# Attention with landmark softmax, then a SiLU MLP: M on 64x32 parts of the array, C v by column halves, and a different order in the first batch

## The chip, the core and the metric

The kernel runs on one core of one Trainium2 chip. The metric is the device time of one execution, in microseconds (us). Engines are named as in the profile: PE is TensorE (matmuls), PEld its weight loads, DVE is VectorE, ACT is ScalarE, POOL is GpSimd. A comparison gives medians, and a ratio with its 95% interval.

## The reference

```python
# B=8 batches, H=8 heads, S=576 tokens, D=64; m=32 landmarks; then an MLP 512 -> 2048 -> 512 on 4608 tokens
q_lm = q.reshape(B, H, m, S // m, D).mean(axis=3)      # k_lm likewise
A  = softmax(q    @ k_lm^T / 8)
Bm = softmax(q_lm @ k_lm^T / 8)
C  = softmax(q_lm @ k^T    / 8)
Z  = Bm^T / (norm1(Bm) * norminf(Bm))
for _ in range(6):
    Z = 2 * Z - Z @ Bm @ Z
attn = A @ Z @ C @ v
h = x @ w_in;  out = (h * sigmoid(h)) @ w_out          # x: attn with the heads side by side
```

## The kernel before

The kernel never forms `attn`. Per batch it makes M, that is (Z C v) of every head times the head's 64 rows of `w_in` (a 32x2048 block for each head), and the first layer is then A times M. The batches overlap: while the first layer of batch b runs (`l1_unit`, tile `h_ps`), the attention of batch b+1 is made in steps between its units, and the second layer (`ops`) of earlier tokens fills in. The tiles `h_ps`, `m_ps` and three of the attention's share a pool of two buffers of two PSUM banks each (`big`); `lm_ps`, `w_ps`, `ns_ps` and others share two buffers of one bank (`small`).

```python
    # v tile: 10 columns blocks of 384; blocks 1..8 are the heads, 0 and 9 are ones (they give the softmax sums)
    vslots = [vp.tile([VP, 10, VI * Dh], BF, ...) for i in range(NV)]
    ...
    idf = constp.tile([128, 128], FP, ...)            # identity in f32, then cast
    nc.vector.memset(idf, 1.0)
    nc.gpsimd.affine_select(out=idf, in_=idf, ...)
    nc.vector.tensor_copy(out=idb, in_=idf)
    ...
    for g in range(NG):                               # selectors, in the pool of lm_ps
        sel_ps = smps.tile([128, 1024], BF, tag="small", name="sel_ps")
        nc.tensor.transpose(out=sel_ps[0:2 * H, 0:128], in_=selm[:, g]..., identity=idb)
        nc.vector.tensor_copy(out=sel[:, g, :], in_=sel_ps[0:2 * H, 0:128])
    ...
    # attn(b): landmark sums of q and k together
        for j in range(J):
            mm(lm_ps[:, 0:256]..., idb, qk[:, :, :, j, :], start=(j == 0), stop=(j == J - 1))
    ...
        def c_times_v(g):                             # once for each half of the heads
            for i in range(VI):
                mm(w_ps[:, 0:320], cts[g][:, i, :], vs[:, 5 * g:5 * g + 5, i * Dh:(i + 1) * Dh], ...)
            nc.scalar.copy(out=wsb[:, g, :], in_=w_ps[:, off:off + 256])
            nc.vector.reciprocal(out=wrec[:, g:g + 1], in_=w_ps[:, so:so + 1])
    ...
        for g in range(NG):                           # M: K=128 rows (two heads, masked), 64 columns
            for f2 in range(2):
                m_ps = big("m_ps")
                for ff in range(2):
                    for p in range(2):
                        mm(m_ps[64 * p:64 * p + 64, ff, :], zt[:, 2 * g + p, :], w_in_sb[:, 2 * g + p, f * 512:(f + 1) * 512])
                nc.scalar.copy(out=m_sb[:, g, f2 * 1024:(f2 + 1) * 1024], in_=m_ps...)
    ...
    def l1_unit(b, dc):
        h_ps = big("h_ps")
        ... 4 matmuls of 288 columns ...
        nc.scalar.activation(out=sig, in_=h_ps[:, :, 0:HS2], func=AF.Tanh, scale=0.5)
        nc.vector.scalar_tensor_tensor(out=gT[...], in0=sig, scalar=1.0, in1=h_ps[:, :, 0:HS2], op0=OP.add, op1=OP.mult)
```

The softmax here doesn't subtract the row's maximum and nothing guards it: scores larger than these inputs give would overflow.

Of the kernel before, what the change touches and what calls it, by code (L numbers as in the profile page):

```python
# [7 lines left out]
FP = mybir.dt.float32  # L8
BF = mybir.dt.bfloat16
AF = mybir.ActivationFunctionType  # L10
OP = mybir.AluOpType
# [4 lines left out]
def kernel(  # L16
# [9 lines left out]
    nc = tc.nc  # L26
    B, H, S, Dh = q.shape
    L = 32
    J = S // L
# [3 lines left out]
    NG = 2  # L33
    VA, VI = 3, 6
    VP = VA * L
# [3 lines left out]
    constp = ctx.enter_context(tc.tile_pool(name="constp", bufs=1))  # L39
    natp = ctx.enter_context(tc.tile_pool(name="natp", bufs=2))  # L40
    vp = ctx.enter_context(tc.tile_pool(name="vp", bufs=1))
    qtp = ctx.enter_context(tc.tile_pool(name="qtp", bufs=2))
    smp = ctx.enter_context(tc.tile_pool(name="smp", bufs=2))
# [9 lines left out]
    def big(nm):  # L53
        return bigp.tile([128, 2, 512], FP, tag="big", name=nm)

    def small(nm):
        return smps.tile([128, 512], FP, tag="small", name=nm)

    def mm(out_ap, lhsT, rhs, start=True, stop=True):
        nc.tensor.matmul(out=out_ap, lhsT=lhsT, rhs=rhs, start=start, stop=stop,  # L60
                         skip_group_check=True)


    w_in_sb = constp.tile([128, 4, DFF], BF, tag="w_in_sb", name="w_in_sb")
    w_out_sb = constp.tile([128, NDC, DMODEL], BF, tag="w_out_sb", name="w_out_sb")
    NV = 2
    vslots = [vp.tile([VP, 10, VI * Dh], BF, tag=f"v{i}", name=f"v{i}") for i in range(NV)]
    qk_t = [None] * B

    def load_qk(b):  # L70
# [7 lines left out]
    def load_v(b):  # L78
        vs = vslots[b % NV]
        for a in range(VA):  # L80
            nc.gpsimd.dma_start(
                out=vs[a * L:(a + 1) * L, 1:9, :],
                in_=v[b].rearrange("h (l a x) d -> a l h (x d)", l=L, a=VA)[a])

    def load_w_in():
        for fc in range(4):
            nc.gpsimd.dma_start(out=w_in_sb[:, fc, :],
                                in_=moe_w_in[fc * 128:(fc + 1) * 128, :])

    def load_w_out():  # L90
        for c in range(4):
# [4 lines left out]
    load_qk(0)  # L96


    idf = constp.tile([128, 128], FP, tag="idf", name="idf")
    nc.vector.memset(idf, 1.0)  # L100
    nc.gpsimd.affine_select(out=idf, in_=idf, compare_op=OP.is_equal, fill=0.0, base=0,
                            pattern=[[-1, 128]], channel_multiplier=1)
    idb = constp.tile([128, 128], BF, tag="idb", name="idb")
    nc.vector.tensor_copy(out=idb, in_=idf)
    hmask = constp.tile([128, 4, L], BF, tag="hmask", name="hmask")
    nc.vector.memset(hmask, 0.0)
    for a in range(4):
# [10 lines left out]
    for g in range(NG):  # L118
        sel_ps = smps.tile([128, 1024], BF, tag="small", name="sel_ps")
        nc.tensor.transpose(out=sel_ps[0:2 * H, 0:128],  # L120
                            in_=selm[:, g].rearrange("p t h -> p (t h)"), identity=idb)
        nc.vector.tensor_copy(out=sel[:, g, :], in_=sel_ps[0:2 * H, 0:128])  # L122
    pmask = constp.tile([128, 2, L], BF, tag="pmask", name="pmask")
    nc.vector.memset(pmask, 0.0)
    for a in range(2):
        nc.vector.memset(pmask[64 * a:64 * (a + 1), a, :], 1.0)
    for i in range(NV):
        nc.vector.memset(vslots[i][:, 0, :], 1.0)
        nc.vector.memset(vslots[i][:, 9, :], 1.0)

    def bc(ap, n, axis):

        shape = list(ap.shape)
        shape.insert(axis, n)
        return ap.unsqueeze(axis).to_broadcast(shape)
# [5 lines left out]
    def attn(b):  # L141
        qk = qk_t[b]
        vs = vslots[b % NV]


        lm_ps = small("lm_ps")
        for j in range(J):
            mm(lm_ps[:, 0:256].rearrange("p (t g d) -> p t g d", t=2, g=NG), idb,
               qk[:, :, :, j, :], start=(j == 0), stop=(j == J - 1))
            if j == 8:  # L150
                yield
        lm = smp.tile([128, 256], BF, tag="lm", name="lm")
        nc.scalar.copy(out=lm, in_=lm_ps[:, 0:256])  # L153

# [3 lines left out]
        def tp(t, g):  # L158
# [4 lines left out]
            else:  # L163
                for c in range(2):
# [8 lines left out]
                                op=OP.mult)  # L173
# [9 lines left out]
        for g in range(NG):  # L183
            for c in range(2):
                mm(sb_ps[:, g * L:(g + 1) * L], LB(0, g, c), LT(1, g, c),
                   start=(c == 0), stop=(c == 1))
# [24 lines left out]
        for g in range(NG):  # L211
# [6 lines left out]
            out=st[:, :, 0:128], in0=f0_ps[:, 0:256].rearrange("p (g x) -> p g x", g=NG),  # L218
            in1=bc(nrm, 128, 2), op=OP.mult)
# [49 lines left out]
        def a_rec_t(rhl):  # L269
            rt_ps = smps.tile([128, 1024], BF, tag="small", name="rt_ps")  # L270
            for ci, (c0, c1) in enumerate(CH):
                n = c1 - c0
                nc.tensor.transpose(out=rt_ps[0:2 * H, c0:c1],
                                    in_=rhl[0:n, ci].rearrange("p t h -> p (t h)"),
                                    identity=idb[0:n, 0:n])
            rt = smp.tile([2 * H, S], BF, tag="rt", name="rt")
            nc.scalar.copy(out=rt, in_=rt_ps[0:2 * H, 0:S])
            return rt

        def a_norm(g, rt):  # L280
            rb = big("rb_ps")
            for hf in range(2):
                mm(rb[:, hf, 0:HS2], sel[:, g, :], rt[:, hf * HS2:(hf + 1) * HS2])
            nc.vector.tensor_tensor(  # L284
                out=etn[:, g, :].rearrange("p (f x) -> p f x", f=2),
                in0=ets[g].rearrange("p (f x) -> p f x", f=2), in1=rb[:, :, 0:HS2], op=OP.mult)

        cts = [None] * NG
# [10 lines left out]
                                 in_=c_ps[0:VP, :, 0:384], func=AF.Exp, scale=sc / J)  # L299
            cts[g] = ct  # L300

        wsb = smp.tile([128, NG, 256], BF, tag="wsb", name="wsb")
        wrec = smp.tile([128, NG], FP, tag="wrec", name="wrec")

        def c_times_v(g):
            w_ps = small("w_ps")
            for i in range(VI):
                mm(w_ps[:, 0:320], cts[g][:, i, :],
                   vs[:, 5 * g:5 * g + 5, i * Dh:(i + 1) * Dh],
                   start=(i == 0), stop=(i == VI - 1))  # L310
            off, so = (64, 0) if g == 0 else (0, 256)
            nc.scalar.copy(out=wsb[:, g, :], in_=w_ps[:, off:off + 256])  # L312
            nc.vector.reciprocal(out=wrec[:, g:g + 1], in_=w_ps[:, so:so + 1])

        st = ns_iter(st, False)
        yield
# [12 lines left out]
        rec = a_sums()  # L329
        st = ns_iter(st, False)  # L330
        yield
        c_times_v(0)
        rt = a_rec_t(rec)
        yield
        st = ns_iter(st, False)
        yield
        a_norm(0, rt)
        c_times_v(1)
        yield
        st = ns_iter(st, True)  # L340
        yield
# [2 lines left out]
        qbd = smp.tile([128, NG, 4, L], BF, tag="qbd", name="qbd")  # L344
        for g in range(NG):
            nc.vector.scalar_tensor_tensor(
                out=qbd[:, g], in0=bc(st[:, g, 128:SW], 4, 1), scalar=wrec[:, g:g + 1],
                in1=hmask, op0=OP.mult, op1=OP.mult)
        zt_ps = small("zt_ps")
        for g in range(NG):  # L350
            for p in range(2):
                mm(zt_ps[:, (2 * g + p) * 64:(2 * g + p + 1) * 64],
                   wsb[:, g, 128 * p:128 * p + 128],
                   qbd[:, g, 2 * p:2 * p + 2, :].rearrange("p a l -> p (a l)"))
        zt = smp.tile([128, 4, 64], BF, tag="zt", name="zt")
        nc.vector.tensor_tensor(  # L356
            out=zt, in0=zt_ps[:, 0:256].rearrange("p (c x) -> p c x", c=4),
            in1=bc(pmask.rearrange("p a l -> p (a l)"), 4, 1), op=OP.mult)
        yield
        m_sb = mp.tile([128, NG, DFF], BF, tag="m", name="m")  # L360
        m_t[b] = m_sb
        for g in range(NG):
            for f2 in range(2):
                m_ps = big("m_ps")
                for ff in range(2):
                    f = 2 * f2 + ff
                    for p in range(2):
                        mm(m_ps[64 * p:64 * p + 64, ff, :], zt[:, 2 * g + p, :],
                           w_in_sb[:, 2 * g + p, f * 512:(f + 1) * 512])
                nc.scalar.copy(out=m_sb[:, g, f2 * 1024:(f2 + 1) * 1024],  # L370
                               in_=m_ps.rearrange("p f x -> p (f x)"))
                yield



# [38 lines left out]


    load_v(0)
    load_w_in()
    load_qk(1)
    load_v(1)
    load_w_out()  # L420
    for _ in attn(0):
        pass
    for b in range(B):
# [12 lines left out]
        for i, u in enumerate(l1):  # L436
            units.append(u)
            want = (i + 1) * len(l2) // len(l1)
            while n2 < want:
                units.append(l2[n2])  # L440
                n2 += 1
        gen = attn(b + 1) if b + 1 < B else iter(())
        NST = 26
        done = 0
# [8 lines left out]
        if b + 2 < B:  # L453
            load_v(b + 2)
# [33 lines left out]
```

## Time and profile before

| kernel before | |
|---|---|
| median of 4 runs | 322.64 us (322.13 to 324.32) |
| span of the profiled run, mean granted clock | 320.7 us, 0.984 |
| PE, DVE, ACT busy | 90%, 64%, 53% |
| M: matmuls, busy | 128 of 512 columns, 21.5 us |
| C v: matmuls, busy | 96 of 320 columns, 16.4 us |

The page of the kernel before. First line: span. Then each engine's busy time with its share and number of instructions; then two rows of the span in 40 slices, busy tenths of PE and the granted clock in tenths; then the chain of waits by engine and by line.

```profile
span 320.7 us, 5155 instructions
PE 287.7 (90%) x2007; PEld 162.4 (51%) x2042; DVE 205.0 (64%) x434; ACT 169.8 (53%) x269; POOL 31.0 (10%) x53
...
PE   0366989989999999999999999999999999999990
...
PEclk9999699999999999999999999999999999999997
...
PE 79%; DVE 11%; ACT 4%; DMA 2%; issue 2%; POOL 0%; ACTq 0%; DVEq 0%; POOLq 0%
PE ops L60 36%; PE h_ps L60 18%; PE m_ps L60 6%; PE lm_ps L60 5%; PE w_ps L60 4%; DVE gT L387 3%; PE c_ps L60 3%; DMA qk<-in_q_dram 2%; PE ns_ps L60 2%; PE sa_ps L60 2%; DVE qT L160 2%; PE rb_ps L60 1%; ACT sig L385 1%; DVE qT L165 1%; DVE lmbd L172 1%
```

PE is at 9 tenths in every slice from the tenth (72 us) on but the last: that stretch is held by PE. The clock has no record before 17.1 us; the row shows that time as full speed, but it was not, as the next timeline tells. M and C v (`m_ps`, `w_ps`) have 6% and 4% of the chain.

Groups of the kernel before. Columns: line, engine, operation, out<-in, rows*columns of the array, shapes, count | busy us, mean ns of one | idle us before, and the releaser.

```profile
L370 ACT CAST m<-m_ps 128x1024 bf16<-128x1024 f32 x32 | 32.2, 1013 | 18.0 <-PE m_ps L60 17.5
...
L60 PE MATMUL m_ps<-w_in_sb,zt 128*64 128x512 bf16 x128 | 21.5, 421 | 0.8 <-DVE zt L356 0.8
...
L60 PE MATMUL w_ps<-v_97,ct 96*128 96x320 bf16 x48 | 8.2, 300 | 0.0
L60 PE MATMUL w_ps<-v_96,ct 96*128 96x320 bf16 x48 | 8.2, 300 | 0.0
```

A mean of 421 ns for an M matmul is a latency, not a cost: matmuls are pipelined. The cost is read from starts. PE's timeline of the kernel before around one M group (start us, duration us, what, count):

```profile
91.17 0.62 PE L60 MATMUL m_ps<-w_in_sb,zt 128*64 128x512 bf16 x4
91.73 0.39 PE L60 MATMUL lm_ps<-qk,idb 128*128 128x256 bf16 x2
```

The group of four starts at 91.17 us and the next matmul at 91.73. In the trace the four starts are 91.172, 91.175, 91.412 and 91.415: two pairs on the two column halves, each pair streaming together.

The head in the timeline of the kernel before:

```profile
9.70 1.38 DVE L160 STREAM_TRANSPOSE qT<-qk 128x1152 bf16<-128x1152 bf16 x1 [0.74 <-DMA qk<-in_q_dram]
...
12.92 0.19 DVE L104 CAST idb<-idf 128x128 bf16<-128x128 f32 x1
...
13.16 0.37 PE L120 MATMUL sel_ps<-idb,selm 128*16 128x128 bf16 x2 [13.16 <-DVE idb L104]
...
13.46 0.34 DVE L122 COPY sel<-sel_ps 16x128 bf16<-16x128 bf16 x2 [0.35 <-PE sel_ps L120]
13.73 3.75 PE L60 MATMUL lm_ps<-qk,idb 128*128 128x256 bf16 x18 [0.20 <-DVE sel L122]
...
19.15 0.26 PE L60 MATMUL sb_ps<-lmT,lmbd 128*128 128x32 bf16 x4 [1.67 <-DVE lmbd L172]
```

The selector transposes on PE need the bf16 identity; its cast stands on DVE behind six transposes which wait for k and q, and so the landmark sums start at 13.73 us. Their starts are 213 ns apart for 256 columns (3.75 us for all 18); later in the same trace such starts are 109 ns apart, so they ran at half the clock.

### The profile page before, as it was taken

How to read it: one execution, taken by the hardware profiler on the slowest of the kernel's cores; microseconds unless marked ns; L12 is line 12 of the kernel's file. 1: busy time of each engine (PE TensorE's matmuls, PEld its weight loads, DVE VectorE, ACT ScalarE, POOL GpSimd, SP SyncE). 2: the span in 40 equal slices, each digit the busy share in tenths (PEclk: the TensorE clock that was granted, in tenths of full speed). 3: DMA queues.
4: the chain of work that ended last, by engine and by line, in shares of the span. 5: the costliest groups of instructions: out<-in, count | busy, mean ns of one | idle time of the engine just before them, and what ended most of it. 6: DMA issues, size and time to landing. Idle time of an engine off the chain costs nothing.

```text
span 320.7 us, 5155 instructions
## 1 busy us (share of the span) xinstructions
PE 287.7 (90%) x2007; PEld 162.4 (51%) x2042; DVE 205.0 (64%) x434; ACT 169.8 (53%) x269; POOL 31.0 (10%) x53
## 2 busy tenths in 40 slices
PE   0366989989999999999999999999999999999990
PEld 0243455546555754666455753666465654555440
DVE  5557589998978696589737794576437663455000
ACT  1041665676557665766474746565645747555110
POOL 7323212100101020000201020000000000000000
PEclk9999699999999999999999999999999999999997
DMA  6999999572168106180617334100011101112122
GB/s 120 209 213 205 205 208 183 73 145 65 37 105 145 53 23 119 48 156 31 106 38 142 86 58 80 49 20 21 29 38 51 46 8 37 55 41 60 50 81 68
DMA packets 18345, 28.13 MB, mean 88 GB/s; under 512 B 912, under 2 KB 9104, under 8 KB 18320
## 3 DMA queue, kind: packets, MB, share of 16 engines
q0 software_dynamic: 13568, 18.35, 33.9%
q1 hardware_dynamic: 4752, 9.44, 10.3%
q8 instruction: 16, 0.26, 0.3%
q14 instruction: 9, 0.07, 0.1%
HBM read 36.70 MB, written 9.44 MB: 144 GB/s over the span
## 4 chain that ended last, share of the span: by engine, by line
PE 79%; DVE 11%; ACT 4%; DMA 2%; issue 2%; POOL 0%; ACTq 0%; DVEq 0%; POOLq 0%
PE ops L60 36%; PE h_ps L60 18%; PE m_ps L60 6%; PE lm_ps L60 5%; PE w_ps L60 4%; DVE gT L387 3%; PE c_ps L60 3%; DMA qk<-in_q_dram 2%; PE ns_ps L60 2%; PE sa_ps L60 2%; DVE qT L160 2%; PE rb_ps L60 1%; ACT sig L385 1%; DVE qT L165 1%; DVE lmbd L172 1%
## 5 line engine op out<-in xcount | busy, mean ns | idle before, releaser
L60 PE MATMUL ops<-w_out_sb,gT 128*128 128x512 bf16 x541 | 143.4, 380 | 1.8 <-issue 0.5
L387 DVE SCALAR_TENSOR_TENSOR gT<-sig,h_ps 128x576 bf16<-128x576 bf16 x128 | 94.7, 746 | 58.9 <-ACT sig L385 58.5
L385 ACT ACTIVATE sig<-h_ps 128x576 bf16<-128x576 f32 x128 | 82.4, 650 | 47.9 <-PE h_ps L60 44.5
L60 PE MATMUL h_ps<-etn,m 128*128 128x288 bf16 x512 | 84.3, 286 | 3.0 <-DVE gT L387 2.6
L60 PEld LDWEIGHTS <-gT 128*128 128x128 bf16 x576 | 53.0, 98 | 46.6 <-issue 8.0
L60 PEld LDWEIGHTS <-m 128*128 128x128 bf16 x512 | 47.6, 97 | 34.0 <-issue 11.3
L370 ACT CAST m<-m_ps 128x1024 bf16<-128x1024 f32 x32 | 32.2, 1013 | 18.0 <-PE m_ps L60 17.5
L403 ACT ACTIVATE ost<-ops 128x512 f32<-128x512 f32 x36 | 21.4, 598 | 24.6 <-PE ops L60 24.4
L165 DVE STREAM_TRANSPOSE qT<-qk 128x576 bf16<-128x576 bf16 x32 | 23.9, 758 | 3.3 <-DMA qk<-in_k_dram 2.1
L233 DVE SCALAR_TENSOR_TENSOR st<-st,ns_ps 128x320 bf16<-128x320 bf16 (+1 forms) x48 | 20.8, 434 | 6.4 <-PE ns_ps L60 6.1
L60 PE MATMUL lm_ps<-qk,idb 128*128 128x256 bf16 x144 | 22.1, 297 | 0.3 <-DVE sel L122 0.2
L160 DVE STREAM_TRANSPOSE qT<-qk 128x1152 bf16<-128x1152 bf16 x16 | 21.7, 1358 | 0.7 <-DMA qk<-in_q_dram 0.7
L60 PE MATMUL m_ps<-w_in_sb,zt 128*64 128x512 bf16 x128 | 21.5, 421 | 0.8 <-DVE zt L356 0.8
L60 PEld LDWEIGHTS <-idb 128*128 128x128 bf16 x144 | 14.6, 105 | 8.3 <-issue 4.0
L298 ACT ACTIVATE ct<-c_ps 96x768 bf16<-96x768 f32 x16 | 12.9, 806 | 7.0 <-PE c_ps L60 7.0
L60 PE MATMUL ns_ps<-st 128*128 128x160 bf16 (+1 forms) x96 | 13.8, 224 | 2.0 <-DVE st L233 1.3
L153 ACT CAST lm<-lm_ps 128x256 bf16<-128x256 f32 x8 | 3.0, 372 | 22.7 <-PE lm_ps L60 22.7
L60 PE MATMUL c_ps<-lmbd,qT 128*96 128x128 bf16 x192 | 14.2, 219 | 0.2 <-ACT et L250 0.2
L60 PEld LDWEIGHTS <-qT 128*96 128x96 bf16 x192 | 13.3, 123 | 1.9 <-issue 0.4
L312 ACT CAST wsb<-w_ps 128x256 bf16<-128x256 f32 x16 | 5.9, 371 | 14.5 <-PE w_ps L60 8.2
L284 DVE TENSOR_TENSOR etn<-et,rb_ps 128x576 bf16<-128x576 bf16 x16 | 12.0, 747 | 1.3 <-PE rb_ps L60 1.1
L250 ACT ACTIVATE et<-sa_ps 128x576 bf16<-128x576 f32 x16 | 10.4, 648 | 4.3 <-PE sa_ps L60 4.2
(81 smaller groups left out, 178.1 us busy)
## 6 DMA issues: line engine op xcount, KB each, us to landing
out_dram<-ost SPq DMA_DIRECT2D x32, 256.0 KB
qk<-in_k_dram POOLq DMA_DIRECT2D x8, 576.0 KB, 6.0
qk<-in_q_dram POOLq DMA_DIRECT2D x8, 576.0 KB, 9.0
v_96<-in_v_dram POOLq DMA_DIRECT2D x12, 192.0 KB, 8.0
v_97<-in_v_dram POOLq DMA_DIRECT2D x12, 192.0 KB, 7.0
w_in_sb<-in_moe_w_in_dram POOLq DMA_DIRECT2D x4, 512.0 KB, 12.9
w_out_sb<-in_moe_w_out_dram POOLq DMA_DIRECT2D x4, 512.0 KB, 16.8
out_dram<-ost SPq DMA_DIRECT2D x8, 128.0 KB
```

What stands on the lines that cost most here:

```text
L60: nc.tensor.matmul(out=out_ap, lhsT=lhsT, rhs=rhs, start=start, stop=stop, skip_group_check=True)
L160: nc.vector.transpose(out=qT[:, 0, g].rearrange("p c j l -> p j c l"), in_=qk[:, 0, g].rearrange("p j (c x) -> p j c x", c=2))
L165: nc.vector.transpose(out=qT[:, 1, g, c].rearrange("p (i a) l -> p a i l", a=VA), in_=qk[:, 1, g].rearrange("p (a i) (c x) -> p a i c x", ...
L233: nc.vector.scalar_tensor_tensor(out=st2[:, :, lo:SW], in0=st[:, :, lo:SW], scalar=2.0, in1=ns_ps[:, 0:NG * SW].rearrange("p (g x) -> p g ...
L250: nc.scalar.activation(out=et.rearrange("p (f x) -> p f x", f=2), in_=sa[:, :, 0:HS2], func=AF.Exp, scale=sc / J)
L284: nc.vector.tensor_tensor(out=etn[:, g, :].rearrange("p (f x) -> p f x", f=2), in0=ets[g].rearrange("p (f x) -> p f x", f=2), in1=rb[:, :, ...
L298: nc.scalar.activation(out=ct.rearrange("p (f x) y -> p f (x y)", f=2), in_=c_ps[0:VP, :, 0:384], func=AF.Exp, scale=sc / J)
L312: nc.scalar.copy(out=wsb[:, g, :], in_=w_ps[:, off:off + 256])
L370: nc.scalar.copy(out=m_sb[:, g, f2 * 1024:(f2 + 1) * 1024], in_=m_ps.rearrange("p f x -> p (f x)"))
L385: nc.scalar.activation(out=sig, in_=h_ps[:, :, 0:HS2], func=AF.Tanh, scale=0.5)
L387: nc.vector.scalar_tensor_tensor(out=gT[:, dc, o:o + S].rearrange("p (f x) -> p f x", f=2), in0=sig, scalar=1.0, in1=h_ps[:, :, 0:HS2], op ...
L403: nc.scalar.activation(out=ost, in_=ops, func=AF.Copy, scale=0.5)
```

## The change

The intents are: M on eight 64x32 parts of the array at once, so that a group of eight matmuls streams once instead of two pairs streaming one after the other; C v on two column halves, so that fewer columns are spent on heads that a row does not need (192 in place of 320); no masking of `zt`; the identity written directly in bf16; and for batch 0 the sums of k ahead of those of q, as k lands first. For the eight parts to be distinct, the second group of heads has its row halves swapped, in `w_in_sb` and in `wsb`. The reciprocal broadcast (tile `rb_ps`, K=16 rows) is the same in both kernels.

```diff
-    vslots = [vp.tile([VP, 10, VI * Dh], BF, ...) for i in range(NV)]
+    vslots = [vp.tile([VP, H, 2, VI * Dh], BF, ...) for i in range(NV)]     # ones behind each head
...
+            if fc < 2: ... as before
+            else:                                                           # row halves swapped
+                for r in range(2):
+                    nc.gpsimd.dma_start(out=w_in_sb[64 * r:64 * r + 64, fc, :],
+                        in_=moe_w_in[fc * 128 + 64 * (1 - r):fc * 128 + 64 * (2 - r), :])
...
-    idf = constp.tile([128, 128], FP, ...)   ... memset, affine_select, tensor_copy to idb
+    idb = constp.tile([128, 128], BF, ...)   ... memset, affine_select
...
-        nc.vector.memset(vslots[i][:, 0, :], 1.0)
-        nc.vector.memset(vslots[i][:, 9, :], 1.0)
+        nc.vector.memset(vslots[i][:, :, 1, :], 1.0)
...
+        if b == 0:
+            for t in (1, 0):
+                for j in range(J):
+                    mm(lmv[:, t], idb, qk[:, t, :, j, :], start=(j == 0), stop=(j == J - 1))
+                yield
+        else: ... as before
...
-        def c_times_v(g): ... 6 matmuls of 320 columns, one copy, one reciprocal; called at two steps
+        def c_times_v():
+            for g in range(NG):
+                for i in range(VI):
+                    for p in range(2):
+                        mm(wv[64 * p:64 * p + 64, g], cts[g][:, i, 64 * p:64 * p + 64],
+                           vsl[:, 8 * g + 4 * p:8 * g + 4 * p + 3, i * Dh:(i + 1) * Dh], ...)
+            nc.scalar.copy(out=wsb[:, 0], in_=wv[:, 0, 0:3:2, :])
+            for r in range(2):
+                nc.scalar.copy(out=wsb[:, 1, r, :], in_=wv[:, 1, 2 - 2 * r, :])
+            nc.vector.reciprocal(out=wrec, in_=wv[:, :, 1, 0])
...
-        zt: 4 matmuls of 64 columns, multiplied by pmask
+        zt: 2 matmuls of 128 columns, copied
...
-        for g in range(NG): for f2 in range(2): ...
+        for f in range(4):
+            m_ps = big("m_ps")
+            for h in range(4):
+                for g in range(NG):
+                    r = 64 * ((h + g) % 2)
+                    mm(m_ps[L * h:L * h + L, g, :], zt[r:r + 64, g, L * h:L * h + L],
+                       w_in_sb[r:r + 64, 2 * g + h // 2, f * 512:(f + 1) * 512])
+            nc.scalar.copy(out=m_sb[:, :, f * 512:(f + 1) * 512], in_=m_ps)
```

More of the change, by code (lines that the diff above doesn't have):

```diff
@@ L66 @@
     NV = 2
-    vslots = [vp.tile([VP, 10, VI * Dh], BF, tag=f"v{i}", name=f"v{i}") for i in range(NV)]
+    vslots = [vp.tile([VP, H, 2, VI * Dh], BF, tag=f"v{i}", name=f"v{i}") for i in range(NV)]
     qk_t = [None] * B
@@ L81, in load_v @@
             nc.gpsimd.dma_start(
-                out=vs[a * L:(a + 1) * L, 1:9, :],
+                out=vs[a * L:(a + 1) * L, :, 0, :],
                 in_=v[b].rearrange("h (l a x) d -> a l h (x d)", l=L, a=VA)[a])
@@ L86, in load_w_in @@
         for fc in range(4):
-            nc.gpsimd.dma_start(out=w_in_sb[:, fc, :],
-                                in_=moe_w_in[fc * 128:(fc + 1) * 128, :])
+            if fc < 2:
+                nc.gpsimd.dma_start(out=w_in_sb[:, fc, :],
+                                    in_=moe_w_in[fc * 128:(fc + 1) * 128, :])
+            else:
+                for r in range(2):
+                    nc.gpsimd.dma_start(
+                        out=w_in_sb[64 * r:64 * r + 64, fc, :],
+                        in_=moe_w_in[fc * 128 + 64 * (1 - r):fc * 128 + 64 * (2 - r), :])
     def load_w_out():
@@ L96 @@
     load_qk(0)
-    idf = constp.tile([128, 128], FP, tag="idf", name="idf")
-    nc.vector.memset(idf, 1.0)
-    nc.gpsimd.affine_select(out=idf, in_=idf, compare_op=OP.is_equal, fill=0.0, base=0,
+    idb = constp.tile([128, 128], BF, tag="idb", name="idb")
+    nc.vector.memset(idb, 1.0)
+    nc.gpsimd.affine_select(out=idb, in_=idb, compare_op=OP.is_equal, fill=0.0, base=0,
                             pattern=[[-1, 128]], channel_multiplier=1)
-    idb = constp.tile([128, 128], BF, tag="idb", name="idb")
-    nc.vector.tensor_copy(out=idb, in_=idf)
     hmask = constp.tile([128, 4, L], BF, tag="hmask", name="hmask")
@@ L122 @@
         nc.vector.tensor_copy(out=sel[:, g, :], in_=sel_ps[0:2 * H, 0:128])
-    pmask = constp.tile([128, 2, L], BF, tag="pmask", name="pmask")
-    nc.vector.memset(pmask, 0.0)
-    for a in range(2):
-        nc.vector.memset(pmask[64 * a:64 * (a + 1), a, :], 1.0)
     for i in range(NV):
-        nc.vector.memset(vslots[i][:, 0, :], 1.0)
-        nc.vector.memset(vslots[i][:, 9, :], 1.0)
+        nc.vector.memset(vslots[i][:, :, 1, :], 1.0)
     def bc(ap, n, axis):
@@ L146, in attn @@
         lm_ps = small("lm_ps")
-        for j in range(J):
-            mm(lm_ps[:, 0:256].rearrange("p (t g d) -> p t g d", t=2, g=NG), idb,
-               qk[:, :, :, j, :], start=(j == 0), stop=(j == J - 1))
-            if j == 8:
-                yield
+        lmv = lm_ps[:, 0:256].rearrange("p (t g d) -> p t g d", t=2, g=NG)
+        if b == 0:
+            for t in (1, 0):
+                for j in range(J):
+                    mm(lmv[:, t], idb, qk[:, t, :, j, :], start=(j == 0), stop=(j == J - 1))
+                yield
+        else:
+            for j in range(J):
+                mm(lmv, idb, qk[:, :, :, j, :], start=(j == 0), stop=(j == J - 1))
+                if j == 8:
+                    yield
         lm = smp.tile([128, 256], BF, tag="lm", name="lm")
@@ L300, in c_scores @@
             cts[g] = ct
-        wsb = smp.tile([128, NG, 256], BF, tag="wsb", name="wsb")
+        wsb = smp.tile([128, NG, 2, Dh], BF, tag="wsb", name="wsb")
         wrec = smp.tile([128, NG], FP, tag="wrec", name="wrec")
-        def c_times_v(g):
+        def c_times_v():
             w_ps = small("w_ps")
-            for i in range(VI):
-                mm(w_ps[:, 0:320], cts[g][:, i, :],
-                   vs[:, 5 * g:5 * g + 5, i * Dh:(i + 1) * Dh],
-                   start=(i == 0), stop=(i == VI - 1))
-            off, so = (64, 0) if g == 0 else (0, 256)
-            nc.scalar.copy(out=wsb[:, g, :], in_=w_ps[:, off:off + 256])
-            nc.vector.reciprocal(out=wrec[:, g:g + 1], in_=w_ps[:, so:so + 1])
+            vsl = vs.rearrange("p h s x -> p (h s) x")
+            wv = w_ps[:, 0:384].rearrange("p (g s d) -> p g s d", g=NG, s=3)
+            for g in range(NG):
+                for i in range(VI):
+                    for p in range(2):
+                        mm(wv[64 * p:64 * p + 64, g], cts[g][:, i, 64 * p:64 * p + 64],
+                           vsl[:, 8 * g + 4 * p:8 * g + 4 * p + 3, i * Dh:(i + 1) * Dh],
+                           start=(i == 0), stop=(i == VI - 1))
+            nc.scalar.copy(out=wsb[:, 0], in_=wv[:, 0, 0:3:2, :])
+            for r in range(2):
+                nc.scalar.copy(out=wsb[:, 1, r, :], in_=wv[:, 1, 2 - 2 * r, :])
+            nc.vector.reciprocal(out=wrec, in_=wv[:, :, 1, 0])
         st = ns_iter(st, False)
@@ L331, in attn @@
         yield
-        c_times_v(0)
+        c_times_v()
         rt = a_rec_t(rec)
@@ L337, in attn @@
         a_norm(0, rt)
-        c_times_v(1)
         yield
@@ L350, in attn @@
         for g in range(NG):
-            for p in range(2):
-                mm(zt_ps[:, (2 * g + p) * 64:(2 * g + p + 1) * 64],
-                   wsb[:, g, 128 * p:128 * p + 128],
-                   qbd[:, g, 2 * p:2 * p + 2, :].rearrange("p a l -> p (a l)"))
-        zt = smp.tile([128, 4, 64], BF, tag="zt", name="zt")
-        nc.vector.tensor_tensor(
-            out=zt, in0=zt_ps[:, 0:256].rearrange("p (c x) -> p c x", c=4),
-            in1=bc(pmask.rearrange("p a l -> p (a l)"), 4, 1), op=OP.mult)
+            mm(zt_ps[:, g * 128:(g + 1) * 128], wsb[:, g].rearrange("p r d -> p (r d)"),
+               qbd[:, g].rearrange("p a l -> p (a l)"))
+        zt = smp.tile([128, NG, 128], BF, tag="zt", name="zt")
+        nc.vector.tensor_copy(out=zt, in_=zt_ps[:, 0:256].rearrange("p (g x) -> p g x", g=NG))
         yield
@@ L361, in attn @@
         m_t[b] = m_sb
-        for g in range(NG):
-            for f2 in range(2):
-                m_ps = big("m_ps")
-                for ff in range(2):
-                    f = 2 * f2 + ff
-                    for p in range(2):
-                        mm(m_ps[64 * p:64 * p + 64, ff, :], zt[:, 2 * g + p, :],
-                           w_in_sb[:, 2 * g + p, f * 512:(f + 1) * 512])
-                nc.scalar.copy(out=m_sb[:, g, f2 * 1024:(f2 + 1) * 1024],
-                               in_=m_ps.rearrange("p f x -> p (f x)"))
-                yield
+        for f in range(4):
[6 more added lines that the diff above has]
+            nc.scalar.copy(out=m_sb[:, :, f * 512:(f + 1) * 512], in_=m_ps)
+            yield
     gT = constp.tile([128, NDC, 2 * S], BF, tag="gT", name="gT")
```

## The prediction

> **What bounds the kernel.** TensorE. The page has PE busy 90% of the span; windows of 20 us show it busy 19.7 to 19.9 of 20 from 80 to 300 us, at a granted clock of 1.00, while DVE and ACT stay at 17 or less. The chain of waits is 79% PE. Only the head differs: before 80 us PE is busy 5.0, 15.7, 17.8 and 18.4 of 20. In the head's timeline PE does nothing until 13.2 us, because the selector transposes wait for the bf16 identity, whose cast sits on DVE behind six transposes that wait for k and q. The landmark sums run 13.7 to 17.5 us (208 ns for 256 columns: half clock).
>
> **M (8 batches).** Before: four groups of four 512-column matmuls. The timeline at 91.2 us shows two 64-column parts starting 3 ns apart and the next pair 237 ns later: 0.43 us of streaming, plus about 0.19 us to enter and leave the mode. The Trainium skill, "TensorEngine Tiling (Array Packing)", Key Properties, says that changing the mode drains the array; this agrees. After: groups of eight on eight distinct 64x32 parts, one stream of 216 ns, about 25 ns of stagger, the same drain. Estimate: 0.62 to 0.43 us a group, 0.75 us a batch.
>
> **C v.** Before 12 matmuls of 320 columns, 135 ns apart: 1.62 us plus gaps. After 12 pairs of 192 columns on two column halves: 12 x 82 ns = 1.0 us, plus one drain of 0.19. Estimate: 0.5 us a batch. Its weight loads should hide, as C's 96-column ones do under 55 ns steps.
>
> **ACT, DVE.** Evictions and the zt copy cost about the same as before. The ones memsets grow from 4 x 384 to 2 x 3072 elements, about 2.6 us each; they end near 7.9 us, which costs little since q's transpose waits for q at 9.7 us.
>
> **Head.** The idea of k sums ahead of q will mostly not pay: lm_ps needs a buffer that the selector copies free, and in the built order these still follow q's first transpose on DVE. So the sums start near 12.0 us, not at k's landing (6.9), last about 3.9 us, and the first Bm scores move from 19.15 to about 17.7. M in the head is bound by ACT's four 1.01 us evictions, but no landmark sums stand between its groups now, and the first h units need only the first eviction: first h_ps near 35 instead of 38.1 us. Head gain: 2.8 us.
>
> **Sum.** Head 2.8 + M 7 x 0.75 + C v 7 x 0.5 = 11.5 us, of which batch 1 and new waits on DVE/ACT keep about 1. Predicted 312.0 us (-3.3%), 308.5 to 316.0. Faster by over 2%: 0.87; within: 0.12; slower: 0.01.
>
> **What would show it.** Eight m_ps starts within about 30 ns, group cost 0.43 us; w_ps pairs 3 ns apart every 82 ns; lm_ps starting at about 12 us after the selector copy; sb_ps at 17.7; first h_ps at 35; PE still saturated from 80 us.
>
> **What would make it wrong.** Eight parts not running together: both row halves write the same PSUM bank, in different partitions, and the skill's page (Gotcha 1) says different row tiles cannot share a bank at once; then M gains nothing or loses. Column-half weight loads not hiding in C v. Or the freed PE time turning into waits for DVE and ACT.

## The result and the profile after

The changed kernel takes 314.89 us (median of 4 runs, 314.19 to 315.74), the kernel before 322.64 us. The ratio is 0.9752, with a 95% interval of 0.9708 to 0.9796. Here and below, a ratio is the mean time of one kernel's runs over that of the other's of the same rounds, so it is not quite the ratio of the medians. Executions over 1.5% slower than the fastest of the same kernel are left out of the means.

The page of the kernel after, the same lines:

```profile
span 312.8 us, 5645 instructions
PE 280.7 (90%) x2268; PEld 161.9 (52%) x2268; DVE 207.4 (66%) x420; ACT 166.8 (53%) x277; POOL 32.0 (10%) x55
...
PE   0465889979999999999999999999999999999990
...
PEclk9998699999999999999999999999999999999997
...
PE 72%; DVE 11%; DMA 8%; ACT 4%; issue 2%; POOL 1%; POOLq 0%; ACTq 0%
PE ops L60 36%; PE h_ps L60 18%; DVE gT L393 5%; DMA v_97<-in_v_dram 4%; PE lm_ps L60 3%; DMA w_in_sb<-in_moe_w_in_dram 3%; PE m_ps L60 3%; PE c_ps L60 2%; ACT sig L391 2%; PE w_ps L60 2%; PE sa_ps L60 2%; PE ns_ps L60 2%; DVE qT L171 2%; PE rb_ps L60 1%; ACT m L377 1%
```

The clock row dips in the fourth and fifth slices; PE is again full from the tenth on, but for the last. On the chain M has 3% and C v 2%, half of what they had.

Groups of the kernel after, with the columns as before:

```profile
L377 ACT CAST m<-m_ps 128x1024 bf16<-128x1024 f32 x32 | 32.1, 1019 | 14.2 <-PE m_ps L60 14.1
...
L60 PE MATMUL m_ps<-w_in_sb,zt 64*32 64x512 bf16 x256 | 13.8, 414 | 1.8 <-ACT m L377 1.0 <-DVE zt L365 0.5 <-DVE gT L393 0.2
...
L60 PE MATMUL w_ps<-v_97,ct 96*64 96x192 bf16 x96 | 5.4, 250 | 0.0
...
L60 PE MATMUL w_ps<-v_96,ct 96*64 96x192 bf16 x96 | 4.7, 248 | 0.0
```

M now has twice as many matmuls, and their busy time falls from 21.5 to 13.8 us; C v falls from 16.4 to 10.1 us. An eviction of M takes as long as before.

PE's timeline of the kernel after around one M group:

```profile
124.20 0.41 PE L60 MATMUL m_ps<-w_in_sb,zt 64*32 64x512 bf16 x8
124.55 0.66 PE L60 MATMUL h_ps<-etn,m 128*128 128x288 bf16 x4
```

Eight matmuls start within 25 ns of each other (124.205 to 124.229 us in the trace), and the next one starts 0.35 us after the first; the kernel before needed 0.56 us for the same work. Both numbers include about 0.1 us to leave the mode.

The head in the timeline of the kernel after:

```profile
6.52 2.62 DVE L129 MEMSET v_97<- 96x3072 bf16 x1 [0.70 <-issue]
...
10.36 1.33 DVE L166 STREAM_TRANSPOSE qT<-qk 128x1152 bf16<-128x1152 bf16 x1
...
12.28 0.30 DVE L127 COPY sel<-sel_ps 16x128 bf16<-16x128 bf16 x2
12.50 3.75 PE L60 MATMUL lm_ps<-qk,idb 128*128 128x128 bf16 x36 [6.35 <-DVE sel L127]
...
17.92 0.27 PE L60 MATMUL sb_ps<-lmT,lmbd 128*128 128x32 bf16 x4 [1.67 <-DVE lmbd L178]
...
33.03 2.10 PE L60 MATMUL lm_ps<-qk,idb 128*128 128x256 bf16 x9
...
34.93 1.17 PE L60 MATMUL h_ps<-etn,m 128*128 128x288 bf16 x4
```

The sums of k do not run ahead: `lm_ps` waits for the selector copies until 12.50 us, when q has landed too. The first Bm scores (`sb_ps`) start at 17.92 us (19.15 before), the first `h_ps` at 34.93 us (38.09 before). Nine of batch 1's landmark sums run just ahead of that `h_ps`, from 33.03 us.

**Where the time came from.** The trace gives the start of each matmul, so both kernels can be cut at the first `h_ps` of each batch:

```
                                         before     after    difference
start to first h_ps of batch 0           38.09      34.93       -3.16
to the first h_ps of batch 1             31.01      32.08       +1.07
six intervals, to that of batch 7       205.00     199.33       -5.67
to the last h_ps                         20.67      20.67        0
```

The first two rows belong together: when the first `h_ps` starts, the kernel after has done only 9 of the 18 landmark sums of batch 1, and the kernel before 13. Head and first interval together gain 2.1 us, and the six intervals gain 5.7 us.

The chain of waits of the kernel after, in order of time (start us, us, what), shows why the first interval gains nothing:

```profile
48.59 0.46 DVE gT L393
...
53.87 0.64 DVE gT L393
54.51 0.66 DVE etn L290
55.17 0.52 DVE qbd L357 x2
55.70 0.69 DVE qT L171
```

These are five of its pieces; from 48.59 to 65 us the chain names hardly anything but DVE. With little second-layer work yet, that interval is a string of DVE work, so PE time saved there is not on the chain. (The same chain, further back, names a landing of `v_97` ahead of `zt_ps` at 29.05 us. `zt_ps` does not read v; the timeline has the multiply that it does read, `qbd` on DVE, ending at 28.99 us. A releaser is inferred, and this one is not it; so the 8% of DMA on the page's chain, which hangs on this step, is no evidence of a wait for v or `w_in`.)

**A ledger of PE in the six intervals.** I split the time between successive matmul starts into three parts: streaming (columns / 2.4 + 2.5 ns, but 26 ns for the matmuls of 4 columns, which start 25 to 26 ns apart; matmuls that start within 8 ns of each other are counted once), short gaps (20 to 125 ns beyond that) and long gaps (over 125 ns). The formula is from the Trainium skill, "TensorE: Matmul & The Clock Gate", Back-to-back issue gap, which gives it for an isolated matmul and says that in a stream with weight loads 128 columns take about 81 ns and 512 about 131; this trace agrees with the formula in its streams as well (216 ns between starts for 512 columns, 122 for 288, 55 for 128). The profile of before lacks 35 of the 576 `ops` matmuls, which would appear as gaps; the kernel of the first experiment lacks none and has the same six intervals to 0.01 us, so it stands in for before.

```
six intervals, us      sum     streaming   short gaps      long gaps     rest
as before             205.01     191.23    10.71 (135)     2.86 (15)     0.21
after                 199.33     182.56    11.78 (133)     4.60 (21)     0.38
difference             -5.68      -8.67    +1.07          +1.74         +0.17
```

Streaming fell by 8.67 us, which with the short gaps makes 7.6 us net, 1.27 us a batch. The long gaps took back 1.74 us. In the timeline of the kernel after, one long gap looks like this:

```profile
124.69 1.01 ACT L377 CAST m<-m_ps 128x1024 bf16<-128x1024 f32 x1 [0.30 <-PE m_ps L60]
...
125.59 0.66 ACT L391 ACTIVATE sig<-h_ps 128x576 bf16<-128x576 f32 x1
...
126.13 0.83 PE L60 MATMUL lm_ps<-qk,idb 128*128 128x256 bf16 x6
...
126.28 0.76 DVE L393 SCALAR_TENSOR_TENSOR gT<-sig,h_ps 128x576 bf16<-128x576 bf16 x1 [2.14 <-ACT sig L391]
...
127.09 0.65 PE L60 MATMUL h_ps<-etn,m 128*128 128x288 bf16 x4
```

The six `lm_ps` matmuls from 126.13 end their streaming at about 126.8, but the next `h_ps` starts at 127.09, 297 ns later than the formula allows. It starts 54 ns after `gT` ends on DVE (126.28 + 0.76), which frees its buffer; `gT` follows `sig` on ACT, and `sig` stood behind M's eviction (124.69 to 125.70). Sorting the long gaps by the ACT or DVE instruction that ended 50 to 59 ns ahead of the matmul, those of `h_ps` on `gT` went from 5 with 1.24 us to 10 with 2.26 us, and those on M's evictions from 2 with 0.26 us to 3 with 0.84 us. So 1.02 us of the added 1.74 us end with `gT` on DVE, and 0.58 us with M's evictions on ACT.

### The profile page after: what moved, and what is told of

Read it like the earlier page. It is cut to its first block, busy times and chain, and to the rows that moved or that the text cites. A ratio compares the mean times of both kernels' runs of the same rounds, so it can differ in the third digit from the quotient of the medians.

```text
span 312.8 us, 5645 instructions
## 1 busy us (share of the span) xinstructions
PE 280.7 (90%) x2268; PEld 161.9 (52%) x2268; DVE 207.4 (66%) x420; ACT 166.8 (53%) x277; POOL 32.0 (10%) x55
## 4 chain that ended last, share of the span: by engine, by line
PE 72%; DVE 11%; DMA 8%; ACT 4%; issue 2%; POOL 1%; POOLq 0%; ACTq 0%
PE ops L60 36%; PE h_ps L60 18%; DVE gT L393 5%; DMA v_97<-in_v_dram 4%; PE lm_ps L60 3%; DMA w_in_sb<-in_moe_w_in_dram 3%; PE m_ps L60 3%; PE c_ps L60 2%; ACT sig L391 2%; PE w_ps L60 2%; PE sa_ps L60 2%; PE ns_ps L60 2%; DVE qT L171 2%; PE rb_ps L60 1%; ACT m L377 1%
## 5 line engine op out<-in xcount | busy, mean ns | idle before, releaser
L60 PE MATMUL ops<-w_out_sb,gT 128*128 128x512 bf16 x576 | 150.6, 379 | 0.1
L60 PE MATMUL lm_ps<-qk,idb 128*128 128x256 bf16 (+1 forms) x162 | 22.2, 289 | 6.3 <-DVE sel L127 6.3
L60 PEld LDWEIGHTS <-idb 128*128 128x128 bf16 x162 | 16.2, 112 | 11.2 <-issue 6.8
L60 PE MATMUL m_ps<-w_in_sb,zt 64*32 64x512 bf16 x256 | 13.8, 414 | 1.8 <-ACT m L377 1.0
L73 POOL DMA_DIRECT2D qk<-in_k_dram x8 | 5.8, 720 | 62.3 <-PE lm_ps L60 45.4
```

The lines of the kernel that those rows point to most:

```text
L60: nc.tensor.matmul(out=out_ap, lhsT=lhsT, rhs=rhs, start=start, stop=stop, skip_group_check=True)
L73: nc.gpsimd.dma_start(out=qk[:, t].rearrange("p g j d -> p g (j d)"), in_=src[b].rearrange("(g h) (l j) d -> (h l) g (j d)", g=NG, l=L))
```

## The experiments

All outputs are right. "Before" is a run of the kernel before on the same chip in the same rounds; its medians were 324.10 us in the first (the first four kernels), 322.75 us in the second (the next four) and 324.15 us in the third. The third ran on another chip than the first two and had no run of the kernel after beside it; there a comparison with after goes by the ratios to before. Intervals of time are read from one profile of each kernel.

### Only the two head parts (head_only)

```diff
 before.py with
-    idf ... tensor_copy(idb, idf)
+    idb = constp.tile([128, 128], BF, ...)  memset, affine_select
-    q and k sums together
+    batch 0: k sums, then q sums
```

> The kernel before with only the two head parts of the change: identity written directly in bf16, and batch 0's k sums ahead of its q sums. In its built order the selector copies stand behind all six transposes on DVE, so lm_ps starts at about 13.2 us (before 13.7). My theory (the head's own gain is small): 0.3 to 0.6 us faster, about 322.1 us. Rival (the head parts carry most of the gain in the head): 2 us or more, lm_ps from 7 us.

Measured: 323.21 us, ratio 0.9982 (0.9949 to 1.0015), the same within noise. `lm_ps` starts at 13.18 us, `sb_ps` at 18.85 us. At these two marks the head parts alone are worth 0.55 and 0.30 us (13.73 and 19.15 us before), as expected; the total can't resolve so little. In the kernel after, `sb_ps` came 1.23 us earlier than before, and the first `m_ps` 1.88 us (29.77 us instead of 31.65); no run isolates what gained the rest.

### Only C v (cv_only)

```diff
 before.py with
+    v slots [VP, H, 2, 384], ones behind each head
+    c_times_v by column halves, called once; wsb evicted in two copies of 128x128
+    zt from 2 matmuls of 128 columns, still masked; M as before
```

> The kernel before with only the v slots and C v by column halves; M as before. Theory A (TensorE is saturated from the third batch on, and single savings add up): C v saves 0.53 us in each of 6 batches and about 1 us in the head: 3.5 to 4.2 us, about 318.7 us. Theory B (saved TensorE time turns into waits for DVE and ACT): 2 us or less, 320.6 us or more.

Measured: 320.25 us, ratio 0.9895 (0.9861 to 0.9929), about 3.4 us. The total fits theory A, but not for its reason: the six intervals give only 1.60 us (203.40 us). Their ledger has 3.68 us less streaming, 1.46 us more short gaps (156 instead of 135) and 0.55 us more long gaps. Going into the column halves and out again is a change of mode on each side, which the full-width C v mostly did not pay. The rest of the gain lies outside these intervals, and no profile places it: in cv_only the first `h_ps` of batch 1 is at 69.69 us, 0.60 us later than in the profile of before (mean clock 0.971 against 0.984) and 0.82 us earlier than in that of head_only (0.973).

### Only M (m_only)

```diff
 before.py with
+    w_in halves swapped; M on eight 64x32 parts; zt copied
-            nc.scalar.copy(out=wsb[:, g, :], in_=w_ps[:, off:off + 256])
+            six copies of 64 partitions a batch, as C v still gives four heads in each row
```

> The kernel before with only M on eight 64x32 parts; C v as before, its result evicted in six part copies a batch. Theory A: 0.81 us in each of 6 batches, and about 1 us in the head: 5 to 6 us, about 317 us. Theory B: the gain is nearer 3 us, because M's faster groups meet the same 1.01 us evictions, so that m_ps and h_ps wait for ACT (gaps above the 96 ns mode change after m_ps).

Measured: 322.58 us, ratio 0.9976 (0.9943 to 1.0009). The total fits neither. In the six intervals it gains 2.98 us (202.03 us): 5.23 us less streaming and 2.05 us more long gaps, which is theory B there. Its head lost what that gained: the first `h_ps` of batch 1 starts at 74.05 us, against 70.51 in head_only. In its profile the clock was halved from 26.41 to 43.48 us (24.66 to 38.31 in head_only), its evictions of `wsb` are more, and its built order has none of batch 1's 18 sums ahead of the first `h_ps`, where before and head_only have 13; which of these cost how much was not separated.

### Four parts in place of eight (four_parts)

```diff
 after.py with w_in and wsb in natural order, and
-            for h in range(4):
-                for g in range(NG):
-                    r = 64 * ((h + g) % 2)
+            for g in range(NG):
+                for h in range(4):
+                    r = 64 * (h % 2)
```

> The kernel after with w_in and wsb in natural order, so that a group of eight M matmuls falls on four parts, twice. If eight parts really stream together, each group costs one stream of 216 ns more: 4 x 8 x 0.216 = 6.9 us of TensorE time more, of which some 5 us should show: about 319.5 us. If the trace's ends only look concurrent and PSUM or the row halves serialise them, nothing is lost: 315 us.

Measured: 319.32 us, ratio 0.9880 (0.9840 to 0.9919). PE's timeline of this kernel:

```profile
91.16 0.61 PE L60 MATMUL m_ps<-w_in_sb,zt 64*32 64x512 bf16 x8
91.71 0.39 PE L60 MATMUL lm_ps<-qk,idb 128*128 128x256 bf16 x2
```

The group takes 0.55 us again, as in the kernel before. The six intervals are 202.97 us, 3.64 us more than after, with 5.31 us more streaming. So the eight parts do stream together, and the swap of the row halves is what the gain of M rests on.

### The changed kernel again (after_again)

> The changed kernel once more, so that the three runs beside it can be held against it on one chip: ratio to before 0.975 as on record, 0.971 to 0.980.

Measured: 315.34 us, ratio 0.9748 (0.9713 to 0.9783). The six intervals are 199.32 us.

### Sums of q and k together again (joint_sums)

```diff
 after.py with
-        if b == 0: k sums, then q sums
+        q and k sums together, as in before.py
```

> The kernel after with batch 0's k and q landmark sums made together again (18 matmuls of 256 columns). My theory: k first buys nothing, because lm_ps waits for the selector copies on DVE until 12.5 us, after q has landed: lm_ps starts at 12.5 us and ends at 16.2 us as in the kernel after, and the time is the same within 0.5 us. Rival (k first is worth its intent): 1 to 2 us slower.

Measured: 314.87 us, ratio 0.9744 (0.9703 to 0.9784); `lm_ps` starts at 12.50 us. Taking k first shows no gain in the kernel as built.

### Selectors in another PSUM pool (sel_other_bank)

```diff
 after.py with
-        sel_ps = smps.tile([128, 1024], BF, tag="small", name="sel_ps")
+        sel_ps = opsp.tile([128, 1024], BF, tag="ops", name="sel_ps")
```

> The kernel after with the two selector transposes in the PSUM pool of the second layer, so that lm_ps need not wait for their copies. If that wait is what holds the sums: k's sums start near 7.0 us, q's near 9.8, lm_ps is done near 12, lmT then waits for DVE's transposes, and the first sb_ps moves from 17.9 to about 15.7 us: 2 us faster than the kernel after, if the clock of the head stays the same. Rival: nothing gained at the end, because what follows waits for data or for DVE.

Measured: 315.19 us, ratio 0.9736 (0.9700 to 0.9771): no clear gain. Yet the timeline of this kernel has what theory asked for:

```profile
6.95 2.08 PE L60 MATMUL lm_ps<-qk,idb 128*128 128x128 bf16 x18 [0.79 <-DMA qk<-in_k_dram]
...
9.80 2.08 PE L60 MATMUL lm_ps<-qk,idb 128*128 128x128 bf16 x18 [0.77 <-DMA qk<-in_q_dram]
...
15.64 0.29 PE L60 MATMUL sb_ps<-lmT,lmbd 128*128 128x32 bf16 x4 [3.77 <-DVE lmbd L178]
```

The sums of k start at 6.95 us and `sb_ps` at 15.64 us, 2.28 us ahead of the kernel after. So the wait for the selector copies was real. The gain is lost later: at the first `sb_ps` of batch 1 it is 1.2 us against the profile of after and 0.9 us against that of after_again. Four of its six timed runs have a granted clock of 0.972 or 0.973 (315.1 to 315.7 us) and two have 0.983 (313.9 and 314.0 us). That pointed at the clock.

### M's eviction on two engines (split_evict)

```diff
 after.py with
-            nc.scalar.copy(out=m_sb[:, :, f * 512:(f + 1) * 512], in_=m_ps)
+            nc.scalar.copy(out=m_sb[:, 0, f * 512:(f + 1) * 512], in_=m_ps[:, 0, :])
+            nc.vector.tensor_copy(out=m_sb[:, 1, f * 512:(f + 1) * 512], in_=m_ps[:, 1, :])
```

> The kernel after with each M eviction of 1.01 us on ACT cut in two halves of about 0.6 us, one on ACT, one on DVE. Theory (part of the saved TensorE time went into waits for two-bank buffers that ACT frees late, behind M's evictions): in the six intervals from the second to the eighth batch's first h_ps the long gaps of TensorE fall from 4.6 us to 3 or less and the intervals' sum from 199.3 by 1 to 2 us. Rival (DVE is the one that frees late): the sum stays or grows, as DVE gets 19 us more work in all.

Measured: 319.26 us, ratio 0.9886 (0.9844 to 0.9928), slower than after. The windows view of the six intervals in the kernel after (stretch in us, its length, busy us and instructions of PE, PEld, DVE, ACT and POOL, clock, DMA share, GB/s):

```profile
67.00:266.33 199.33, 198.10 (x1636) 113.54 (x1636) 141.04 (x288) 122.56 (x204) 11.15 (x18) 1.00 0.32 66
```

The same view of split_evict:

```profile
70.68:271.36 200.68, 199.24 (x1638) 113.38 (x1637) 158.67 (x314) 114.31 (x205) 11.17 (x18) 1.00 0.34 69
```

DVE has 17.6 us more work, and the sum grows by 1.36 us; the long gaps grow from 4.60 to 5.90 us. My theory is not borne out: relief for ACT at DVE's cost makes it worse. That agrees with DVE's `gT` as the link that cannot be delayed, but the edit changes both engines at once and does not isolate it. Most of the loss is elsewhere: in the profile the first `h_ps` of batch 1 is at 70.68 us, 3.68 us later than in after, with the clock halved from 31.17 to 38.00 us and again from 65.31 to 68.72 us; what cost how much there was not separated. PE reads as busy 99% in both, because the busy time includes the modelled tail of each matmul; gaps of 0.2 us hide in that number, and only the starts show them.

### Unread matmuls in batch 0 (warm)

```diff
 after.py with, in batch 0 only,
+        warm(n, rhs): n matmuls of idb with rhs into an unused PSUM tile that nobody reads
+            2 before the sums' copy, 3 after each Newton step (rhs = st),
+            3 before zt, 2 after each of M's first two evictions (rhs = that part of M)
```

> The kernel after with 30 matmuls in batch 0 whose results nobody reads, between the Newton steps and behind M's evictions, only to keep TensorE busy. Theory (the head is also held by the half clock from 29.0 or 29.5 to 36 us): the clock stays at 1.00 from about 16 us on, the first sb_ps of the third batch comes 1 to 1.5 us earlier, about 314 us, with less spread between runs. Rival: the head is held by chains of waits, not by the clock, and the extra matmuls cost 0.5 us or more.

Measured: 314.14 us, ratio 0.9702 (0.9662 to 0.9741). The clock row of its page (granted clock in tenths, 40 slices):

```profile
PEclk9999999999999999999999999999999999999997
```

The same row of the page of sel_other_bank, with its dip in the fourth and fifth slices:

```profile
PEclk9998799999999999999999999999999999999997
```

(The trace has 27 unread matmuls, not the 30 of the expectation.) The records of the clock have 1.00 from 17.68 us to the end of the work, where the kernel after has 0.50 from 29.50 to 36.33 us. Five of six runs took 313.8 to 314.6 us. The first `sb_ps` of the third batch came at 62.19 us (62.91 and 62.57 in the two profiles of after), so 0.4 to 0.7 us earlier, less than the 1 to 1.5 us expected. Theory and rival are both partly right: the clock returns something, and the extra matmuls cost something (`zt_ps` starts at 29.76 us, against 28.78 in after, whose clock is still 1.00 then).

### Both (sel_warm)

> The kernel with the selectors in another PSUM bank (first sb_ps at 15.6 us, yet only 0.3 us gained in all) plus the same unread matmuls. If the half clock ate what that kernel won by 15.6 us, both together are 2.5 to 3.5 us faster than the kernel after: about 312 us. Rival: 314.5 us or more, the early start is lost to something else.

The edit is that of sel_other_bank and that of warm (7 unread matmuls after the sums instead of 2). Measured: 311.73 us (311.61 to 312.89), ratio 0.9625 (0.9589 to 0.9661). Its interval lies clear below that of after_again (0.9713 to 0.9783), so it beats both kernels. Its clock is 1.00 from 13.21 us on, `sb_ps` starts at 15.64 us, and the first `sb_ps` of the third batch at 60.00 us, 2.6 to 2.9 us ahead of after. In the same place sel_other_bank alone was 0.9 to 1.2 us ahead (61.68 us) and warm alone 0.4 to 0.7. The early start pays once the clock holds, so the half clock did eat part of the gain of sel_other_bank. It shows in one place: from the first to the last start of batch 1's 18 landmark sums, with a few `h_ps` between, sel_other_bank takes 4.05 us and sel_warm 2.36 us. (sel_warm has five more unread matmuls than warm, and its clock rises earlier, at 13.21 us instead of 17.68; how much of the sum comes from that was not tested.)

### The broadcast over 128 rows (rb_full)

```diff
 after.py with
-    sel = constp.tile([2 * H, NG, 128], ...);  rt = smp.tile([2 * H, S], ...)
+    sel = constp.tile([128, NG, 128], ...);    rt: two tiles of [128, S]; rows 16 to 127 zeroed once
```

> The kernel after with the reciprocal broadcast over K=128 rows (rows 16 to 127 zero) in place of K=16. If the gaps of 0.09 us on each side of rb_ps are changes of the array's mode, they vanish: 22 gaps of 2.1 us in six batches, so the six intervals fall from 199.3 to about 197.5 us, and the time by about 2 us. Rival: these gaps are waits for rt or for buffers, and stay.

Measured: 315.17 us, ratio 0.9711 (0.9666 to 0.9755); one of its six runs was slow (318.85 us, clock 0.958) and is left out of the ratio. The six intervals are 197.66 us, 1.67 us less than after, and their short gaps fall from 11.78 to 10.08 us, so these gaps were changes of mode. But the total is not clearly better, because the first `h_ps` of batch 1 starts at 68.70 us (67.00 in after). The built order around batch 0's end differs (four `h_ps` ahead of all 18 sums of batch 1); whether that is the cause was not tested.

### All three (all_three)

> The three edits together (other bank, unread matmuls, K=128 broadcast): if they add up, 4 to 5 us faster than the kernel after, about 310 to 311 us, and faster than both kernels.

Measured: 311.86 us, ratio 0.9622 (0.9581 to 0.9664): faster than both kernels, not distinguished from sel_warm, and not the sum of the parts. Its runs at a clock of 0.993 took 310.4 to 311.2 us, the other three (0.985 to 0.989) 312.5 to 313.4 us; in its profile the clock was halved from 29.09 to 35.92 us in spite of the unread matmuls.

## Why the prediction was right, and which terms were off

The forecast was 312.0 us with a range of 308.5 to 316.0 and "faster"; 314.89 us lies in the range, and the direction was right. The gain was 7.8 us where the sum said 10.5.

- **M.** Right. A group fell from 0.56 to 0.35 us between starts, eight parts within 25 ns; predicted was 0.62 to 0.43 us with the entry counted. The stated risk, two row halves that write one PSUM bank, did not come true. four_parts shows that the time really depends on the eight parts. Streaming of M alone fell by 5.23 us in six batches, 0.87 us a batch; predicted 0.75 net.
- **C v.** Nearly right. Pairs start 3 ns apart every 82 ns, as predicted. In cv_only the net of streaming and mode changes is 2.2 us in six batches, 0.37 us a batch against 0.5, since its group pays 21 more short gaps.
- **Together** they gave 1.27 us a batch on PE, against the 1.25 of the sum. The step was right; the term after it was not.
- **"Of which batch 1 and new waits on DVE/ACT keep about 1."** This is the mis-sized term. The first interval kept all of batch 1's 1.25 us, because that interval is DVE's; and the long gaps in the six intervals kept another 1.74 us. The mechanism was named in the prediction, and its size was about three times as large. That most of the waits end with DVE's `gT` is inferred from end times 50 to 59 ns ahead of the matmul; split_evict, which loads DVE and makes the gaps longer, agrees but does not isolate it.
- **Head.** The reading was close in each mark: `lm_ps` at 12.50 (predicted 12.0), `sb_ps` at 17.92 (17.7), first `h_ps` at 34.93 us (35). The ones memsets were mis-sized: they ended at 9.14 us (predicted 7.9), and q's first transpose started at 10.36 us instead of 9.70. The k sums showed no gain in joint_sums. The last mark was hit partly by luck. The path was another one: the first `h_ps` did not follow the first eviction of M, which ended at about 31.5 us, but came behind all four groups of M and nine sums of batch 1. And the mark moves with the clock: in the profile of joint_sums, where the clock was halved from 24.76 to 38.41 us, it is at 37.48 us. It was also the wrong place to read the gain: half of batch 1's sums were still to come after it, and at the third batch's first `sb_ps` 2.1 us were left of the 2.8.
- **What the prediction did not see.** The clock. In both kernels it is halved during batch 0, from about 29 to 36 us in the two profiles of after and from 30.76 to 37.58 in that of before, and which run has a longer stretch differs: runs of before in the third call are 322.0 to 322.5 us at a clock of 0.984 to 0.988, and 323.9 to 325.5 us at 0.972 or 0.973. That is a spread of 2 us which no change of the code made.

## What to carry to other kernels

Small matmuls on distinct parts of the array do stream together, and a layout that makes the parts distinct is worth a swap of rows; count a change of mode (about 0.09 us on each side) for every group, and group them. PE time that is saved turns into time only where PE is what the chain runs on, so cost the stretches separately, and ask which buffer the faster matmuls will wait for next. Before moving work to an earlier place, look in the built order for the buffer it reuses, and look at the granted clock of that stretch: here an earlier start paid only once PE was kept busy.

## What the Trainium skill lacked or had wrong

- "TensorEngine Tiling (Array Packing)", Key Properties, says that changing the mode drains the array, without a size. Here a group with another shape costs about 0.09 to 0.10 us on each side (ops to `m_ps` 21 times, 1.99 us in all), and a matmul over K=16 rows pays it as well: with 128 rows the short gaps fell by 1.7 us in six batches.
- The same page, Gotcha 1, says that different row tiles cannot access the same PSUM bank at the same time. Here both row halves write each of the two banks, in different partitions; the eight matmuls start within 25 ns, the group takes 0.35 us between starts, and the result is correct. For different partitions the measurement decides against the page.
- "TensorE: Matmul & The Clock Gate", Part 1, says in its table that the clock falls to half after an idle window of about 3.4 us; further down, in "A second HAM failure mode", it tells of falls with short idles alone, without saying how short or how many. The lengths agree (the half-clock stretch of after is 6.83 us, twice that), but no idle window was needed. The windows view of the kernel after, for the two windows before the fall and the two at half clock (columns as above):

```profile
22.68:26.09 3.41, 2.41 (x43) 1.96 (x44) 1.99 (x7) 0.68 (x4) 1.29 (x2) 1.00 1.11 212
26.09:29.50 3.41, 1.54 (x10) 0.67 (x9) 2.71 (x8) 0.33 (x1) 0.19 (x1) 1.00 1.21 203
29.50:32.91 3.41, 2.12 (x32) 0.54 (x32) 3.41 (x6) 2.42 (x3) 2.58 (x4) 0.50 1.27 206
32.91:36.33 3.42, 3.42 (x24) 2.28 (x17) 1.99 (x3) 1.54 (x3) 0.58 (x1) 0.50 1.23 204
```

  PE was busy for 1.54 of 3.41 us in the window before the fall, in bursts. In the same kernel the window from 15.85 to 19.26 us, with 1.74 us busy, was followed by none, and in joint_sums one with 2.17 us busy (21.35 to 24.76 us) was followed by a fall; so PE's busy time in one window does not tell it.
